# One joined load for both layouts of v, and fillers in the first halves only: linear attention, a token-mixing block and a gated block on one core

## The chip, the cores and the metric

The kernel runs on one core of a Trainium2 chip. Its engines work side by side, each through its own list of instructions: TensorE (matmuls; PE in the profile, PEld its weight loads), VectorE (DVE), ScalarE (ACT), GpSimd (POOL), and SyncE (SP), which issues the transfers. The metric is the device time of one execution in microseconds; lower is better.

## The reference, cut to what matters

Three blocks follow each other, for a batch of 4, 8 heads of 48 (384 channels) and 768 positions, all in float32:

```python
f = 1.0 / (1.0 + np.exp(-f_logit))
for t in range(S):                                   # per batch and head
    state = f[t][:, None] * state + outer(k[t], v[t])
    y[t] = q[t] @ state
theta = x @ w_theta                                  # x: y, heads side by side
y = w_tok_r @ (x * cos(theta)) + w_tok_i @ (x * sin(theta))
u = x + y
x2 = u + maximum(u @ w_ch, 0)
h = maximum(x2 @ w_in, 0)                            # 1024 wide: u, v
out = (u * (w_spatial @ layer_norm(v) + b_spatial)) @ w_out
```

## The kernel before

**Attention in chunks.** The recurrence is worked out in 12 chunks of 64 positions. A unit `u` is a pair of heads of one batch; there are 4 units in a batch, 16 in all. For a unit, `att_w` (or `half_w`) makes the outer products of k and v per chunk (tile `pw`), VectorE scans them into the state after each chunk (`cu`, later `cb`), `att_s` makes the scores of q and k inside each chunk (tile `psc`), which VectorE masks into `sc`, and `att_x` (or `half_x`) adds q times the state and the masked scores times v (tile `px`) and writes the result X. Every fourth row of the head pairs' tiles carries dimensions of a fourth pair, which are gathered by transfers into `kp` and `qp`; the fourth unit of each batch reads those.

v is needed in two layouts: with 128 positions on the partitions for the outer products (`VN`, tile names vn0 and vn1, from the array `vu`), and with 64 positions of either head of the pair for px (`VC`, vc0 and vc1, from `va`). Each layout has two tiles that alternate over units, and each is loaded by a transfer of its own: `half_load` (two transfers of 144 KB) and `att_load` (two of 288 KB).

**The first batch in halves.** Units 0 to 3 are worked on in two halves of 384 positions (h = 0 and h = 1), so that the work starts when half of the data is there: decay products on VectorE and ScalarE, transposes of k (tile `pt`), then `half_att`. Before each half's px, `warm` puts four matmuls of the identity (fillers, `px<-ident`) on TensorE; at the start 16 more (`pt<-ident`). A float32 matmul shows as two records, so a group of four fillers is eight records, and the eight groups are 64. The fillers' results are not used.

**Mixing and the rest.** `p1_theta` makes theta (`pth`), `p1_z` its sines and cosines times X (`z`), `p1_acc` multiplies by the token weights (`acc`), `p1_h` by w_ch (`hh`). Token weights arrive in twelve loads of 768 KB into a tile `ws` of two buffers (`ws<-tok_dram`), which ScalarE and VectorE convert to float32 (`tk`); w_theta comes through the same tile (`ws<-wt_dram`, converted into `ft`). From about 348 us on the gated block runs, batch by batch (`pv`, `pu`, `pg`, `po`).

**What sets the order.** Everything up to about 348 us is planned: the program's instructions are numbered as units in the order in which they are written (a whole group of matmuls is one unit), and the table `LINE` gives for each engine (T, V, A, G, and Q for SP's queue) the order in which it does its units. An engine works through its list strictly in that order, so an instruction that waits holds all behind it. A semaphore wait is added for each dependence on another engine. All data transfers of the planned stretch go through the one queue of SP. All instructions are recorded under line 259, in the helper that calls the engine; tiles tell them apart.

Of the kernel before, what the change touches and what calls it, by code (L numbers as in the profile page):

```python
# [10 lines left out]
F32 = mybir.dt.float32  # L11
# [10 lines left out]
P = 128  # L22
# [58 lines left out]
    ],  # L81
# [18 lines left out]
    ],  # L100
# [19 lines left out]
    ],  # L120
# [1247 lines left out]
```

## Time and profile before

| | before |
|---|---|
| median of 3 runs | 595.83 us (594.65 to 596.77) |
| profiled execution, its own time | 598.03 us |
| its span, first to last instruction | 596.3 us |
| TensorE busy | 581.0 us, 97% |
| VectorE busy | 452.0 us, 76% |
| ScalarE busy | 352.8 us, 59% |
| GpSimd busy | 29.1 us, 5% |
| granted TensorE clock, mean | 0.997 of full speed |

The span is what the trace covers; the profiled execution's own time has 1.7 us more around it. The profiled execution is one run, the median is over others. Busy shares are means over stages with different limits, and TensorE's records overlap, since the ends of matmuls are modelled: the start of one record to the start of the next says more than the length of one.

### The profile page before, as it was taken

Reading aid. Unit: us, or ns where it says so; the run is one execution under the profiler, and the core shown is the slowest. Engines: PE = TensorE matmul, PEld = TensorE weight load, DVE = VectorE, ACT = ScalarE, POOL = GpSimd, SP = SyncE. Lnnn points to the kernel's source line nnn. Section 1 sums busy time; section 2 is a strip of 40 time slices with the busy share of each in tenths; the row PEclk is TensorE's granted clock in tenths of the full one; section 3 lists DMA queues with packets and bytes.
Section 4 is the critical chain, followed back from the end, with each engine's and each line's share of the span. In section 5 each row is a group of like instructions: output and inputs, shape, how many; then the busy total and the mean of one; then the engine's idle time right before and its main releaser. Section 6 shows DMA issues by size and latency. Waiting matters only on the chain.

```text
span 596.3 us, 14184 instructions
## 1 busy us (share of the span) xinstructions
PE 581.0 (97%) x5750; PEld 533.3 (89%) x5750; DVE 452.0 (76%) x816; ACT 352.8 (59%) x683; POOL 29.1 (5%) x95
## 2 busy tenths in 40 slices
PE   7899998999999999999999999999999999999995
PEld 6776676877999999999999989999999999999995
DVE  6898998899887777764868587983968396839681
ACT  7798896598877888754664146623642364246421
POOL 5320110000000000000000000000000000000000
PEclk9999999999999999999999999999999999999998
DMA  7779966686978887778789999896049604940422
GB/s 240 209 240 333 281 200 250 226 287 210 304 240 307 271 311 247 256 249 282 244 282 320 338 354 299 288 373 212 1 139 373 203 1 147 371 145 0 158 89 78
DMA packets 68585, 139.44 MB, mean 234 GB/s; under 512 B 6496, under 2 KB 40800, under 8 KB 68512
## 3 DMA queue, kind: packets, MB, share of 16 engines
q1 hardware_dynamic: 68368, 138.36, 68.9%
q8 instruction: 47, 0.77, 0.6%
q14 instruction: 26, 0.21, 0.1%
q10 hardware_dynamic: 144, 0.10, 0.1%
HBM read 104.20 MB, written 31.85 MB: 228 GB/s over the span
## 4 chain that ended last, share of the span: by engine, by line
PE 91%; DMA 3%; DVE 2%; issue 1%; ACT 1%; SPq 1%; POOL 0%; DVEq 0%; ACTq 0%; POOLq 0%
PE acc L259 27%; PE pg L259 15%; PE po L259 9%; PE pu L259 8%; PE pv L259 8%; PE hh L259 6%; PE pth L259 6%; PE px L259 3%; PE psc L259 3%; PE pw L259 2%; PE pt L259 2%; DMA ws<-tok_dram 1%; SPq L259 1%; DMA k<-kd_dram 1%; DVE icp L259 1%
## 5 line engine op out<-in xcount | busy, mean ns | idle before, releaser
L259 PE MATMUL acc<-tk,z 128*128 128x384 f32 x792 | 172.4, 369 | 0.0
L259 PEld LDWEIGHTS acc<-tk,z 128*128 128x128 f32 x792 | 138.3, 189 | 15.8
L259 PE MATMUL pg<-sp,vn 128*128 128x384 f32 x504 | 88.0, 336 | 0.0
L259 PEld LDWEIGHTS pg<-sp,vn 128*128 128x128 f32 x504 | 87.4, 188 | 0.0
L259 PE MATMUL po<-wo,gt 128*128 128x384 f32 x288 | 51.3, 338 | 0.0
L259 PEld LDWEIGHTS po<-wo,gt 128*128 128x128 f32 x288 | 50.8, 188 | 0.0
L259 PE MATMUL pu<-x,wi 128*128 128x384 f32 x288 | 50.7, 335 | 0.0
L259 PEld LDWEIGHTS pu<-x,wi 128*128 128x128 f32 x288 | 50.1, 188 | 0.3
L259 PE MATMUL pv<-wi,x 128*128 128x512 f32 x216 | 49.8, 390 | 0.0
L259 PEld LDWEIGHTS pv<-wi,x 128*128 128x128 f32 x216 | 40.5, 188 | 8.2
L259 PE MATMUL hh<-uT,wc 128*128 128x384 f32 x216 | 41.9, 341 | 0.6 <-DVE uT L259 0.4
L259 ACT ACTIVATE gt<-g 128x384 fp32r<-128x384 f32 x32 | 16.7, 523 | 43.1 <-DVE g L259 42.5
L259 PEld LDWEIGHTS hh<-uT,wc 128*128 128x128 f32 x216 | 37.7, 188 | 1.6 <-DVE uT L259 0.9
L259 DVE TENSOR_TENSOR vn<-vr,vn 128x768 fp32r<-128x768 f32 x24 | 22.9, 955 | 16.1 <-ACT vn L259 15.8
L259 ACT ACTIVATE vn<-vr 128x768 fp32r<-128x768 f32 x24 | 20.2, 844 | 20.4 <-PE pg L259 17.9
L259 PE MATMUL pth<-wh,xT 128*128 128x384 f32 x108 | 31.9, 350 | 0.0
L259 DVE BATCH_NORM_STATS2 st<-vr 128x6 f32<-128x512 f32 x24 | 16.1, 687 | 19.6 <-ACT vr L259 19.6
L259 PE MATMUL px<-vc,sc 64*64 64x48 f32 x768 | 27.1, 220 | 0.2
L259 ACT ACTIVATE ws<-ws 128x768 f32<-128x768 f32 (+2 forms) x28 | 20.7, 738 | 10.4 <-DMA ws<-wo_dram 4.2
L259 ACT ACTIVATE oo<-po 128x384 f32<-128x384 f32 (+1 forms) x24 | 11.6, 482 | 24.8 <-PE po L259 23.7
L259 ACT ACTIVATE sn<-sn 128x384 f32<-128x384 f32 x48 | 24.3, 520 | 2.9 <-DVE sn L259 2.7
L259 PEld LDWEIGHTS px<-vc,sc 64*64 64x64 f32 x768 | 24.7, 140 | 0.5 <-DMA vc<-va_dram 0.3
(141 smaller groups left out, 1055.0 us busy)
## 6 DMA issues: line engine op xcount, KB each, us to landing
sp<-wpd SPq DMA_DIRECT2D x56, 576.0 KB, 5.9
tk<-tkp SPq DMA_DIRECT2D x48, 384.0 KB, 5.0
ws<-tok_dram SPq DMA_DIRECT2D x12, 768.0 KB, 5.9
tkp<-tk SPq DMA_DIRECT2D x24, 384.0 KB, 5.0
tkd<-tk SPq DMA_DIRECT2D x12, 384.0 KB, 5.7
x2d<-xt SPq DMA_DIRECT2D x24, 192.0 KB, 4.5
ws<-tkd SPq DMA_DIRECT2D x12, 384.0 KB, 4.9
xs<-x2d SPq DMA_DIRECT2D x12, 384.0 KB, 3.9
```

The source lines that it names most:

```text
L259: r = f(*a, **k)
```

## The change

The two tiles of v become one tile `VW` for each of the two buffers, of [128, 2, 12, 48]: the second index is the half of the positions; of the twelve slots, 0 to 5 hold the layout for the outer products (three position blocks for each head of the pair), 6 to 11 the layout for px (six chunks). The host-side array `vw` holds both layouts in that order, so that a half load and a whole load are one transfer each (288 KB and 576 KB), of one contiguous stretch per partition. The number of issues falls by 20 (8 half loads and 12 whole loads), the bytes stay the same.

`half_x` calls `warm` only for h = 0, so that four groups of fillers out of eight are gone.

The table `LINE` is a new one: 24 numbers fewer (20 loads, 4 groups of fillers), all later numbers shifted, and another order. Matched unit by unit, its lists hold the same remaining units on every engine. The mean shift of a unit is about two places on TensorE, four on VectorE, on ScalarE and in SP's queue. In the part up to the end of the second halves, what changes most is:

| unit | place before | place after |
|---|---|---|
| SP: loads of k, second halves, units 1 and 2 | 33, 39 | 17, 18 |
| SP: three loads of w_theta | 18, 23, 35 | 11, 23, 32 |
| SP: first three loads of token weights | 43, 45, 58 | 36, 37, 48 |
| SP: load of v for unit 2, first half (vn; vc) | 19; 27 | 21 (joined) |
| SP: load of v for unit 3, first half (vn; vc) | 30; 31 | 31 (joined) |
| ScalarE: first conversion step of tok loads 1, 2, 3 | 74, 84, 96 | 64, 74, 89 |
| VectorE: the three later steps of tok load 1 | 62, 63, 65 | 59, 60, 64 |
| VectorE: mask of unit 3, first half | 37 | 40 |
| TensorE: token matmuls of the first batch ahead of the last half px | 2 groups | 4 groups |

On TensorE the first group of fillers goes behind unit 0's scores, where it stood ahead of them. The diff, with the table's lines left out but for the start of the lists of T and Q:

```diff
 LINE = {
     "T": [
-        45, 46, 47, 48, 49, 50, 51, 52, 53, 61, 54, 55, 56, 57, 82, 58, 59, 60, 95, 100, 91, 101, 121, 128, 132, 137, 144, 138, 148, 153, 154, 159,
+        45, 46, 47, 48, 49, 50, 61, 51, 52, 53, 54, 82, 55, 56, 57, 58, 59, 60, 94, 90, 99, 100, 120, 126, 130, 135, 141, 136, 145, 150, 151, 155,
...
     "Q": [
-        13, 65, 14, 66, 15, 104, 125, 88, 67, 89, 105, 106, 126, 172, 64, 193, 232, 30, 141, 86, 173, 84, 35, 63, 124, 87, 142, 123, 85, 157, 158,
+        13, 65, 103, 14, 66, 15, 88, 168, 189, 67, 30, 105, 104, 124, 226, 64, 190, 227, 169, 170, 139, 63, 35, 123, 86, 122, 315, 85, 84, 87, 154,
...
-        self.VN = [a1.tile([P, 2, NT, D], F32, name=f"vn{i}") for i in range(2)]
-        self.VC = [a1.tile([P, NC, D], F32, name=f"vc{i}") for i in range(2)]
+        self.VW = [a1.tile([P, 2, NC, D], F32, name=f"vw{i}") for i in range(2)]
...
     def half_load(self, u, h):
         w = u % 2
-        self.Q.dma_start(out=self.VN[w][:, :, 3 * h : 3 * h + 3], in_=self.a["vu"][u][:, :, 3 * h : 3 * h + 3])
-        self.Q.dma_start(out=self.VC[w][:, 6 * h : 6 * h + 6], in_=self.a["va"][u][:, 6 * h : 6 * h + 6])
+        self.Q.dma_start(out=self.VW[w][:, h], in_=self.a["vw"][u][:, h])
...
-        Q, sc, v, st = self.att_kq(u)[1], self.SC[u % 2], self.VC[u % 2], self.st[u, h]
+        Q, sc, v, st = self.att_kq(u)[1], self.SC[u % 2], self.VW[u % 2], self.st[u, h]
         ps = [self.bank("px") for _ in range(2)]
-        self.warm(ps[0])
+        if h == 0:
+            self.warm(ps[0])
...
-                T.matmul(o, lhsT=sc[r, C * c : C * c + C], rhs=v[r, c], start=(c == 0), stop=True)
+                T.matmul(o, lhsT=sc[r, C * c : C * c + C], rhs=v[r, c // 6, 6 + c % 6], start=(c == 0), stop=True)
...
-        self.T.matmul(out, lhsT=self.KT[r, o : o + (C - 1) * step + 1 : step], rhs=self.VN[u % 2][r, i, n], start=True, stop=True)
+        self.T.matmul(out, lhsT=self.KT[r, o : o + (C - 1) * step + 1 : step], rhs=self.VW[u % 2][r, n // 3, 3 * i + n % 3], start=True, stop=True)
...
     def att_load(self, u):
         w = u % 2
-        self.Q.dma_start(out=self.VN[w], in_=self.a["vu"][u])
-        self.Q.dma_start(out=self.VC[w], in_=self.a["va"][u])
+        self.Q.dma_start(out=self.VW[w], in_=self.a["vw"][u])
...
+    rows = v2.reshape(B * NP, 2, 2, NT // 2, P, D).transpose(0, 4, 2, 1, 3, 5).reshape(B * NP, P, 2, NT, D)
+    cols = v2.reshape(B * NP, 2, 2, NC // 2, C, D).transpose(0, 1, 4, 2, 3, 5).reshape(B * NP, P, 2, NC // 2, D)
...
-        "vu": c(v2.reshape(B * NP, 2, NT, P, D).transpose(0, 3, 1, 2, 4)),
-        "va": c(v2.reshape(B * NP, 2, NC, C, D).transpose(0, 1, 3, 2, 4).reshape(B * NP, P, NC, D)),
+        "vw": c(np.concatenate([rows, cols], 3)),
```

## Rows read from the trace of the kernel before

**Rows 1.** Stretches: us, busy us and count by engine, granted clock, DMA share, GB/s.
```profile
30.00:55.00 25.00, 23.62 (x408) 17.77 (x407) 22.92 (x35) 21.19 (x49) 3.45 (x10) 1.00 0.82 282
55.00:100.00 45.00, 43.44 (x750) 30.58 (x751) 43.31 (x59) 38.22 (x71) 5.81 (x12) 1.00 0.82 269
100.00:348.00 248.00, 247.64 (x2780) 230.58 (x2776) 186.83 (x278) 166.28 (x293) 5.76 (x23) 1.00 0.81 272
```

**Rows 2.** TensorE's waits, whole span: us together, times, the longest.
```profile
PE px L259 <- DVE cu L259: 2.4, 4, 1.2
...
PE psc L259 <- issue: 1.6, 1, 1.6
```

**Rows 3.** Timeline of TensorE: start us, us, form, count [idle before, releaser].
```profile
2.33 3.88 PE L259 MATMUL pt<-ident 128*128 128x128 f32 x18 [2.33 <-POOL ident masks.py:199]
...
13.77 0.30 PE L259 MATMUL px<-vc,sc 64*64 64x48 f32 x8
...
29.80 1.06 PE L259 MATMUL px<-ident 128*128 128x128 f32 x8
30.71 2.20 PE L259 MATMUL pth<-ft,xt 128*128 128x384 f32 x6
33.02 0.39 PE L259 MATMUL px<-cu,qp 64*64 64x48 f32 x8
...
38.48 1.05 PE L259 MATMUL px<-ident 128*128 128x128 f32 x8
39.47 0.39 PE L259 MATMUL px<-cu,qp 64*64 64x48 f32 x8
...
43.63 1.05 PE L259 MATMUL px<-ident 128*128 128x128 f32 x8
44.90 0.39 PE L259 MATMUL px<-cu,qp 64*64 64x48 f32 x8 [0.21 <-DVE cu L259]
...
50.07 1.05 PE L259 MATMUL px<-ident 128*128 128x128 f32 x8
51.05 0.39 PE L259 MATMUL px<-cu,qp 64*64 64x48 f32 x8
...
54.84 0.55 PE L259 MATMUL pt<-ident,k 128*128 128x128 f32 x3 [0.59 <-ACT X L259]
```

**Rows 4.** The chain that ended last: start us, us, what.
```profile
35.26 0.86 PE psc L259 x22
...
43.09 7.06 DMA ws<-tok_dram
```

**Rows 5.** Timeline of SP's queue: issue start us, its us, transfer.
```profile
5.62 0.43 SPq L259 DMA_DIRECT2D vc<-va_dram  x1
...
11.71 0.57 SPq L259 DMA_DIRECT2D vn<-vu_dram  x1
...
17.37 0.53 SPq L259 DMA_DIRECT2D vc<-va_dram  x1
...
48.10 0.40 SPq L259 DMA_DIRECT2D vc<-va_dram  x1
```

**Rows 6.** Timeline of VectorE: start us, us, form [idle before, releaser].
```profile
29.74 0.36 DVE L259 TENSOR_SCALAR ft<-ws 128x384 uint32<-128x384 uint32 x1 [0.31 <-ACT ws L259]
...
31.63 0.56 DVE L259 TENSOR_TENSOR k<-k,icp 128x384 f32<-128x384 f32 x1 [0.35 <-DMA k<-kd_dram]
32.11 0.85 DVE L259 TENSOR_TENSOR_SCAN cu<-cu 128x336 f32<-128x336 f32 x1
...
41.32 0.96 DVE L259 SCALAR_TENSOR_TENSOR tk<-ws,tk 128x768 uint32<-128x768 uint32 x1
...
51.11 0.56 DVE L259 TENSOR_SCALAR tk<-ws 128x768 uint32<-128x768 uint32 x1 [1.26 <-ACT ws L259]
```

**Rows 7.** DMA issues: transfer, count, KB each, median us to landing.
```profile
vc<-va_dram SPq DMA_DIRECT2D x12, 288.0 KB, 5.8
...
vc<-va_dram SPq DMA_DIRECT2D x8, 144.0 KB, 4.0
```

More of the change, by code (lines that the diff above doesn't have):

```diff
@@ L619, in att_x @@
         A, T, pr = self.A, self.T, u % NP
-        Q, sc, v, st = self.att_kq(u)[1], self.SC[u % 2], self.VC[u % 2], self.st[u]
+        Q, sc, v, st = self.att_kq(u)[1], self.SC[u % 2], self.VW[u % 2], self.st[u]
         ps = [self.bank("px") for _ in range(2)]
@@ L630, in att_x @@
                 r = slice(64 * i, 64 * i + 64)
-                T.matmul(o, lhsT=sc[r, C * c : C * c + C], rhs=v[r, c], start=(c == 0), stop=True)
+                T.matmul(o, lhsT=sc[r, C * c : C * c + C], rhs=v[r, c // 6, 6 + c % 6], start=(c == 0), stop=True)
         for i in range(2):
```

121 rows, old and new, of the table LINE are left out of this document.

## The prediction

> **What bounds the kernel now.** First the page's slices, then the stretches of [rows 1]. From 100 us on TensorE is busy 247.64 of 248 us, and from 55 to 100 us 43.44 of 45: there the time is the sum of TensorE's instructions. Before 55 us it is another kernel: from 30 to 55 us TensorE is busy 23.62, VectorE 22.92 and ScalarE 21.19 of 25 us, and they hand small pieces to each other. This change takes nothing out of TensorE's work after 55 us, so what it brings is what the stretch before 55 us becomes shorter, less what waits a new order makes later.
>
> Then TensorE's waits: all that the profile names are small, 2.4 us for VectorE's scans (cu) in four waits and 1.6 us with no releaser, in one [rows 2], 2.3 us at the very start and 0.59 us for ScalarE's X [rows 3]. So little is to be had from waits; but TensorE's busy time before 55 us holds fillers, which do no work. The chain [rows 4] says what set the pace there: TensorE's own work from 35.26 us, then the third tok load, issued at 43.09 us and landing 7.06 us later; behind it come ScalarE's conversion and a table load, and at 54.84 us the transpose [rows 3] from which TensorE runs nearly without a gap. TensorE's timeline [rows 3] shows the fillers of the second halves and what follows each, SP's queue [rows 5] the issues, and VectorE's timeline [rows 6] where VectorE stood still.
>
> **The change, part by part.**
>
> *Fillers of the second halves.* Four groups go, each four matmuls (eight records). From the start of a group to that of its successor [rows 3]: 30.71 - 29.80 = 0.91 us, 39.47 - 38.48 = 0.99, 44.90 - 43.63 = 1.27 less the wait of 0.21 = 1.06, and 51.05 - 50.07 = 0.98; 3.94 us together. What of it is on the path:
> - First group: the theta matmuls behind it come 0.91 us earlier, but the px behind those began at 33.02 us, when the scan of VectorE that ran from 32.11 to 32.96 us was done [rows 3, 6]. I take 0; ends 0 and 0.91.
> - Second: its px ran at once, and the chain lies on TensorE from 35.26 to 43.09 us [rows 4]. I take 0.99; ends 0 and 0.99.
> - Third: its px waited for a scan, so TensorE gains only what VectorE is ahead by then. VectorE stood still for 0.31 us (for the conversion of w_theta) and 0.35 us (for k's load) at 29.7 and 31.6 us [rows 6]; both loads are issued earlier now (below), so 0.66 us, say 0.7. Ends 0 and 1.06.
> - Fourth: its px ran at once, 0.98, but the transpose at 54.84 us waited 0.59 us for ScalarE [rows 3], which came late through the third tok load [rows 4]. So 0.98 counts only if that load is earlier too. Ends 0 and 0.98.
>
> *One load in place of two.* 20 issues go from SP's queue. Nine of them are vc loads before 50 us, 0.43, 0.43, 0.53, 0.55, 0.43, 0.43, 0.53, 0.38 and 0.40 us of issue, 4.1 us together (the first, one of the dearest and the last stand in [rows 5]). The joined half load has the size of a whole load of before, 288 KB, which for vc took 5.8 us to landing where a half took 4.0 [rows 7], so the outer products' v may land 1.8 us later. What hides it: among TensorE's waits none of pw for a load of v is named, and the first unit's pw has the start fillers before it. Cover gone, it would be 1.8 us once, at the start.
>
> *The queue's new order.* The second-half loads of k go from places 33 and 39 to 17 and 18, the w_theta loads come a little earlier, the first three tok loads from 43, 45 and 58 to 36, 37 and 48. The third tok load needs the buffer that the first one's conversion frees (41.32 + 0.96 = 42.28 us, [rows 6]); its conversion on ScalarE stands ten places earlier, the three steps on VectorE three, three and one. In before VectorE then stood still for 1.26 us until 51.11 us [rows 6]: as much can the load come earlier before another thing is late. That removes ScalarE's lateness: 0.59 us of TensorE's wait at 54.84, and the fourth filler's 0.98 counts.
>
> *A wait that is added.* The joined tile is free only when px of two units earlier is done; the old vn only needed pw. For unit 2 the vn load went out at 11.71 us, vc at 17.37 us [rows 5]; unit 0's px began its last eight at 13.77 us and ended at 14.07 [rows 3]. In the new list this load stands at place 21; 20 issues at some 0.5 us, with a wait for the first product of q between, bring SP there at about 12 us (an estimate from [rows 5]: before, the 19th goes out at 11.71 us). SP then waits about 2.1 us, and behind it stand the gathers of kp, the second w_theta load and the gathers of qp. But at 14.1 us SP had in before issued 22 entries, two of them vc loads; the new list has 20 issued then. So the queue is level, and VectorE now has three more instructions (a product, a first step of the conversion, a scan) ahead of the mask that needs kp, together nearly 2 us by the like of them in [rows 6]. I take 0; ends 0 and 2.1 us of loss.
>
> *The order elsewhere.* The planned stretch is reshuffled to 348 us (mean shift two places on TensorE, four on VectorE and ScalarE). What it could gain there is the idle time of TensorE, 1.56 us from 55 to 100 and 0.36 us to 348 [rows 1]. What it could lose is new waits while VectorE has 1.7 us of slack in 45 us [rows 1]; the dearest price at hand for a late VectorE is 2.4 us in four waits [rows 2]. I take 0 from ends of 1.9 gained and 2.4 lost.
>
> Sum: 0 + 0.99 + 0.7 + 0.98 + 0.59 = 3.26, say 3.3 us. The profiled execution took 598.03 us (span 596.3 and 1.7 us around it), which is 2.2 us over the median 595.83 of the runs; the sum gives it 594.7 us, and the median 592.5 us.
>
> **The clock, which speaks against the change.** The granted clock reads 1.00 (2.4 GHz) in all stretches from 30 to 348 us [rows 1]. What the lower of the two levels, 1.2 GHz, costs can be seen at the very start: 18 filler records took 3.88 us, 0.216 us each, where the eight at 29.80 us took 0.114 us each [rows 3]. The Trainium skill (TensorE: Matmul & The Clock Gate, Part 1: The HAM clock gate) says that the throttled state is the default one and that only TensorE's activity keeps the clock up; by it a stretch emptied of fillers is where the clock could fall. The trace agrees in its first records. In the stretch concerned TensorE is busy 23.62 of 25 us [rows 1]; without 3.9 us of fillers 19.7 us of dense small matmuls and wide theta matmuls are left, so I expect it to hold.
>
> **The rivals.**
> - *VectorE sets the pace.* It is busy 22.92 of 25 us from 30 to 55 us [rows 1], and runs from 31.63 to 49.85 us back to back (27 instructions; [rows 6] has the first and the standstill at the end). If it doesn't get ahead, the fillers' time turns into TensorE's waits for scans: the second counts half, the others nothing, and the tok load alone gives 0.59. Gain up to 1.8 us, say 1.1: 594.7 us. For it: two of the four px waited for a scan. Against it: VectorE's own standing still of 0.31, 0.35 and 1.26 us came from loads, which all go out earlier.
> - *More is gained.* All of 3.94 and the 0.59, 4.5 us, and part of the 1.56 us that TensorE stands still between 55 and 100 us: under 591.3 us. For it: 1.6 us of that is a wait for nothing that the profile names [rows 2], so another order may be without it. Against it: the first group's time is had only with an earlier scan.
> - *The joined load holds the queue* (the other side). Place: unit 2's load at place 21 of SP's queue, and again unit 3's. Price: 2.1 us. It decides from the point where kp lands later than now by more than the nearly 2 us of work that VectorE has ahead of unit 3's mask; VectorE then stands still and all that follows is later. With the filler terms lost to the same late VectorE: 595.83 + 2.1 = 597.9 us. Against it: the count of entries above.
> - *The clock falls* in one stretch between two removed groups: from 29.80 to 38.48 us that is 8.7 us of work at half pace, 8.7 us more: 592.5 + 8.7 = 601.2 us.
> - *The change doesn't do what it says* can't well be: the fillers and the issues are instructions that are no longer there.
>
> **How the numbers follow.** A difference under 0.3% (1.8 us here) can't be told from none: faster means under 594.0, slower over 597.6. Forecast (gain of 1.8 to 4.5 us): 0.52, at 592.5. More gained: 0.10. VectorE sets the pace: 0.24, at 594.7, just inside "same". Queue held: 0.09, and clock: 0.05, both slower. So faster 0.62, same 0.24, slower 0.14. The forecast's own range is 591.3 to 594.0. For 8 in 10 the range goes down into the larger gain (all terms at their good ends, 3.94 + 0.59 + 1.56 = 6.1 us, give 589.7) to 590.2, and up over VectorE's case and some new waits (594.7 and most of the 2.4 us that new waits may cost) to 596.6; the slower cases and the last end of the larger gain are left out.
>
> **What would show it.** Right: px<-ident with 32 records in place of 64; the third tok load issued by 41.8 us or earlier; the transpose of k that came at 54.84 us about 3 us earlier against the work done by then; granted clock 1.00 from 30 to 55 us; TensorE's waits before 55 us no larger together than before. Wrong: TensorE's waits for cu grown by 2 us or more (VectorE's case); SP idle from 12 to 14 us and VectorE idle behind it before 27 us (the queue's); records between 30 and 50 us at twice their pitch (the clock's); or a gain at 55 us that is gone by 348 us, given back as new waits between 55 and 200 us, which is what I know least about.

## The result and the profile after

The changed kernel is slower: 599.79 us median (598.86 to 601.44, 6 runs) beside 596.3 us for the kernel before on the same chip (594.65 to 597.05, 6 runs), a ratio of 1.0065, 95% interval 1.0043 to 1.0086. Forecast was 592.5 us; the range to 596.6 us does not hold it. The profiled execution took 599.35 us, its span 597.5 us.

The stretches first, of the changed kernel, with two short ones around 254 us added (columns as in [rows 1]):

```profile
30.00:55.00 25.00, 24.46 (x408) 17.05 (x401) 23.99 (x36) 20.66 (x47) 2.74 (x15) 1.00 0.79 284
55.00:100.00 45.00, 43.92 (x841) 30.84 (x840) 42.52 (x60) 39.12 (x72) 3.53 (x8) 1.00 0.73 246
100.00:348.00 248.00, 244.24 (x2667) 228.50 (x2665) 184.49 (x275) 164.50 (x290) 11.41 (x22) 0.99 0.79 269
248.00:254.60 6.60, 4.40 (x130) 3.71 (x133) 2.51 (x4) 1.65 (x4) 0.00 (x0) 1.00 0.98 339
254.80:258.00 3.20, 3.20 (x69) 3.08 (x65) 1.36 (x1) 1.09 (x3) 0.00 (x0) 0.50 1.04 409
```

From 30 to 100 us TensorE is busier than in [rows 1], with 32 filler records fewer. From 100 to 348 us it is busy 244.24 us where it was 247.64, and at 254.80 us its granted clock is 0.50, the lower of its two levels. Its waits over the whole span say what came in (us together, times, the longest; before: [rows 2]):

```profile
PE pw L258 <- DMA vw<-vw_dram: 2.4, 2, 2.2
...
PE px L258 <- DVE cu L258: 1.5, 3, 0.6
PE pt L258 <- DVE k L258: 1.2, 1, 1.2
PE hh L258 <- DVE xt L258: 1.0, 1, 1.0
PE acc L258 <- DVE tk L258: 1.0, 2, 0.8
PE acc L258 <- DMA tk<-tkp: 0.8, 1, 0.8
```

The first, hh's, the larger of tk's and tkp's lie at 251, 351, 134 and 222 us, where the kernel before has no wait above 0.4 us. The fillers' places, on TensorE's timeline (before: [rows 3]):

```profile
30.15 2.20 PE L258 MATMUL pth<-ft,xt 128*128 128x384 f32 x6
...
32.61 0.39 PE L258 MATMUL px<-cu,qp 64*64 64x48 f32 x8
...
39.92 0.39 PE L258 MATMUL px<-cu,qp 64*64 64x48 f32 x8
...
50.72 0.39 PE L258 MATMUL px<-cu,qp 64*64 64x48 f32 x8
...
53.96 0.82 PE L258 MATMUL pt<-ident,k 128*128 128x128 f32 x6
```

No px waits for a scan at the three places shown, and the third tok load is issued at 40.40 us (43.09 in [rows 4]). So far this looks like the forecast. The wait at 251 us, first on TensorE, then in SP's queue:

```profile
250.24 1.31 PE L258 MATMUL acc<-tk,z 128*128 128x384 f32 x6
253.73 1.69 PE L258 MATMUL pw<-vw,kt 64*64 64x48 f32 x48 [2.18 <-DMA vw<-vw_dram]
```

```profile
232.60 0.38 SPq L258 DMA_DIRECT2D X<-wp_dram  x1
242.24 0.49 SPq L258 DMA_DIRECT2D qp<-q  x1
...
246.79 0.38 SPq L258 DMA_DIRECT2D vw<-vw_dram  x1
```

The joined load of unit 15 stands behind a gather of qp, which reads a product that VectorE ends only at 242.21 us:

```profile
241.26 0.95 DVE L258 TENSOR_TENSOR q<-q,cw 128x768 f32<-128x768 f32 x1
```

Issued at 246.79 us, the load lands 6.9 us later. In before the vn load of that unit went out ahead of its gather, and only vc came later:

```profile
237.01 0.42 SPq L259 DMA_DIRECT2D vn<-vu_dram  x1
...
243.28 0.49 SPq L259 DMA_DIRECT2D qp<-q  x1
...
244.98 0.41 SPq L259 DMA_DIRECT2D vc<-va_dram  x1
```

The wait at 351 us is one of VectorE's order (its timeline, then TensorE's):

```profile
349.99 0.56 DVE L258 TENSOR_TENSOR wt<-X 128x384 f32<-128x384 f32 x1 [0.86 <-DMA wpd<-X]
350.58 0.56 DVE L258 TENSOR_TENSOR X<-X 128x384 f32<-128x384 f32 x1
...
351.81 0.55 DVE L258 SCALAR_TENSOR_TENSOR xt<-hh,xt 128x384 f32<-128x384 f32 x1
```

```profile
352.41 0.80 PE L258 MATMUL hh<-uT,wc 128*128 128x384 f32 x3 [1.03 <-DVE xt L258]
```

VectorE stands at an instruction that needs a transfer, and the addition for which TensorE waits is queued behind it.

**Where the lead went.** Let each TensorE record other than fillers count with the mean start-to-start time of its kind (steps in which the engine stood idle left out); both kernels then have the same work. Against the profile of before, the changed kernel begins the same work earlier (-) or later (+) by, in us:

```
us in before      55     100     240     260     340     360
changed         -3.5    -4.8    -3.4    +0.3    +0.3    +1.5
```

The two kernels do the work in different orders, so the first figures hang on the weights: with medians in place of means it is 4.1 us ahead at 55 us and 2.9 at 240; from 260 us on nothing changes. So the changed kernel is 3.5 to 4.1 us ahead at 55 us, where 3.3 were forecast; 3.2 to 3.7 us go between 240 and 260 us (2.2 of wait, the rest at half clock) and about 1.2 at 351 us. One caution, which the experiments bear out: before's profile lies 1.7 us over its median, and the changed one had, as it turned out, the best start of all its kind.

### The profile page after: what moved, and what is told of

It reads as the page before. It is cut to its first block, busy times and chain, and to the rows that moved or that the text cites. A ratio compares the mean times of both kernels' runs of the same rounds, so it can differ in the third digit from the quotient of the medians.

```text
span 597.5 us, 14081 instructions
## 1 busy us (share of the span) xinstructions
PE 578.3 (97%) x5718; PEld 529.9 (89%) x5718; DVE 450.9 (75%) x816; ACT 354.1 (59%) x683; POOL 33.9 (6%) x95
## 4 chain that ended last, share of the span: by engine, by line
PE 76%; DMA 10%; DVE 5%; ACT 4%; issue 1%; SPq 1%; POOL 0%; ACTq 0%; DVEq 0%
PE acc L258 19%; PE pg L258 15%; PE po L258 8%; PE pu L258 8%; PE pv L258 8%; PE hh L258 5%; PE pth L258 4%; PE px L258 3%; DMA vw<-vw_dram 2%; PE psc L258 2%; DMA wpd<-X 2%; DMA ws<-tok_dram 2%; PE pw L258 2%; PE pt L258 2%; DVE tk L258 1%
## 5 line engine op out<-in xcount | busy, mean ns | idle before, releaser
L258 PE MATMUL px<-vw,sc 64*64 64x48 f32 x768 | 27.2, 220 | 0.0
L258 DVE TENSOR_TENSOR z<-sn,z 128x768 fp32r<-128x768 f32 x18 | 17.2, 956 | 12.6 <-ACT z L258 12.5
```

Of the source, the lines that this page charges most:

```text
L258: r = f(*a, **k)
```

## The experiments

Each was timed against the kernel before on its own chip, so ratios can be compared and bare medians less well (v15_look2 and v15_look3 are one execution each). "Old order" and "new order" are the tables `LINE` of the two kernels.

| kernel | median us | ratio to before, 95% interval |
|---|---|---|
| changed kernel | 599.79 | 1.0065, 1.0043 to 1.0086 |
| nofill_old | 596.80 | 0.9997, 0.9980 to 1.0014 |
| after_fill | 603.45 | 1.0102, 1.0082 to 1.0122 |
| joined_old | 600.98 | 1.0064, 1.0046 to 1.0082 |
| after_v15 | 600.77 | 1.0059, 1.0037 to 1.0081 |
| v15_look2, v15_look3 | 598.78, 599.79 | one execution each |
| hybrid | 596.92 | 0.9999, 0.9979 to 1.0019 |
| hybrid84 | 601.26 | 1.0092, 1.0065 to 1.0120 |
| newlate | 604.59 | 1.0138, 1.0115 to 1.0162 |
| after_split | 613.28 | 1.0295, 1.0270 to 1.0320 |
| after_fix | 597.87 | 1.0019, 0.9998 to 1.0040 |
| fix_no15 | 600.14 | 1.0062, 1.0041 to 1.0082 |
| v15_351 | 598.91 | 1.0043, 1.0022 to 1.0065 |
| after_fix2 | 596.13 | 0.9983, 0.9960 to 1.0005 |
| fix_fill | 597.55 | 1.0008, 0.9994 to 1.0023 |
| fix_split | 596.64 | 0.9994, 0.9978 to 1.0011 |
| fix2_split | 595.22 | 0.9984, 0.9967 to 1.0001 |
| split_start | 594.18 | 0.9947, 0.9926 to 0.9967 |

**The two edits alone, in the old order.** nofill_old takes the four groups of fillers out and nothing else:

```diff
-        self.warm(ps[0])
+        if h == 0:
+            self.warm(ps[0])
```

> The kernel before with its own order and its two loads of v; only the four groups of fillers of the second halves are gone. Theory 1 (the fillers' time is gained before 55 us, and the new kernel loses it again later to new waits): a gain of 1 to 3.3 us, 593.0 to 595.3 us, since the second group's 0.99 us lies on TensorE's chain and the others need earlier loads. Theory 2 (VectorE sets the pace before 55 us and the fillers were cover): 595.5 to 597 us, TensorE's waits for the scans grown by about what the fillers took.

Measured 0.9997, with 0.17% (1.0 us) either way: none of the 2.7 us that the prediction's sum gives to the fillers can be seen. Its waits from 10 to 56 us and the four px on its TensorE show why (before: [rows 2, 3]):

```profile
PE px L249 <- DVE cu L249: 4.2, 6, 1.2
```

```profile
33.23 0.39 PE L249 MATMUL px<-cu,qp 64*64 64x48 f32 x8 [0.26 <-DVE cu L249]
...
39.45 0.39 PE L249 MATMUL px<-cu,qp 64*64 64x48 f32 x8 [0.58 <-DVE cu L249]
...
45.23 0.39 PE L249 MATMUL px<-cu,qp 64*64 64x48 f32 x8 [1.22 <-DVE cu L249]
...
50.55 0.39 PE L249 MATMUL px<-cu,qp 64*64 64x48 f32 x8
```

The first three px begin at 33.23, 39.45 and 45.23 us where they began at 33.02, 39.47 and 44.90: the fillers' time became waits for VectorE's scans. The fourth runs at once, 0.50 us earlier. The transpose of k that waited 0.59 us for ScalarE in before runs without a wait here, 0.87 us earlier, though the third tok load goes out later than in before (43.40 us, and 43.09): it lands after 5.4 us where it took 7.06 [rows 4].

joined_old keeps the old order and the fillers and joins the loads, each at vn's place or, where the tile is not free then, behind the px that frees it:

```diff
-        self.Q.dma_start(out=self.VN[w], in_=self.a["vu"][u])
-        self.Q.dma_start(out=self.VC[w], in_=self.a["va"][u])
+        self.Q.dma_start(out=self.VW[w], in_=self.a["vw"][u])
```

> The kernel before with its own order and all fillers, but with the joined load of v in place of the two, each at the old vn load's place, or behind the px that it has to wait for (nine of twenty are moved back so). Theory 3 (the joined load itself costs, because it is free only after px of two units earlier): unit 13's load can go out only at 176.8 us in place of 156.1, for outer products at 178.6 us; with 5.8 us to landing they are 4 us late, so 598.5 to 601 us. Theory 1 in the form that the new order's places alone make the late waits: 595.5 to 597 us.

Measured 0.64% or 3.8 us slower (1.1 either way). The unit that waits is unit 11, counted in the program (the expectation calls it 13). Its load can only go out once px of unit 9 has read the tile, and pw, which used to need vn alone, waits 3.32 us (TensorE, then the stretch behind it):

```profile
181.42 1.69 PE L248 MATMUL pw<-vw,kt 64*64 64x48 f32 x48 [3.32 <-DMA vw<-vw_dram]
```

```profile
182.00:184.90 2.90, 2.90 (x45) 2.72 (x38) 0.00 (x0) 1.70 (x4) 0.00 (x0) 0.50 0.96 339
```

The clock stands at 0.50 right behind this wait too.

**The fillers in the new order.** after_fill puts one group ahead of each of the four second-half px of the changed kernel (`warm` for both halves, and its four units in the list of T).

> The changed kernel with the four groups of fillers put back, each right ahead of its px; all else as changed. Theory 1: 2 to 4 us slower than the changed kernel's 599.8, so 601.8 to 603.8 us. Theory 2: the same as the changed kernel within 0.6 us, 599.2 to 600.4 us.

0.37% or 2.2 us slower than the changed kernel (1.7 either way), as if the fillers cost their time there. But its profile has waits of 1.4 to 1.6 us at 185, 256 and 353 us, far behind the fillers; fix_fill (below) is the same edit with some of the waits of this order taken away.

**The largest wait.** after_v15 moves unit 15's load ahead of the gather:

```diff
 "Q": ...
-        1386, 1496, 1156, 1139, 1155, 1171, 1170, 1189, 1186,
+        1386, 1496, 1189, 1156, 1139, 1155, 1171, 1170, 1186,
```

> The changed kernel with one load moved: unit 15's joined load of v goes out ahead of the gather of q (which waits until 242.2 us) in place of five places behind it. Theory 1: TensorE's wait of 2.2 us for that load at 251.5 us is gone and the time falls by about as much, 597.0 to 598.2 us. Rival: TensorE's next instructions wait for other late things there (token weights, the store of the gated block's weights at 352 us), 599.2 to 600.4 us.

The wait and the half clock are gone from its profile, which took 596.5 us, but that was the lowest of nine executions, and the median did not fall. Two more profiles of the same program:

> The changed kernel with unit 15's load moved ahead, a second profile of the same program, since its first one was the fastest of its executions. Theory D': another wait of 1 us or more, or the clock at half for 3.4 us, stands in it at a fixed place (600 to 602). Theory E': the places differ from one execution to the next.

> A third profile of the same program. Same expectations as for the second: one fixed place with Theory D', differing places with Theory E'.

Both kinds of thing stand in them: fixed places (0.8 and 0.7 us for tk at 136 us, 1.1 us for xt at 350 us in both) and things that differ. The same TensorE record, at 22.10 us in the first profile, begins 0.6 and 0.8 us later; and in v15_look2 alone the granted clock is 0.50 from 27.99 to 31.40 us, behind waits of 0.6, 0.9 and 0.5 us.

**Mixed orders.** hybrid and hybrid84 follow the new order to TensorE's 60th and 84th entry, then the old one; newlate is the mirror of hybrid; after_split is the new order whole; all four with two loads per unit. hybrid against the new order, in the numbering with two loads:

```diff
 "T": ...
-        409, 446, 293, 432, 340, 342, 386, 431, 411,
+        409, 446, 293, 431, 386, 340, 342, 432, 344,
...
```

> The new order up to the 60th unit of TensorE's list (the last group of two-sided products of the first image, about 51 us; the other four lists are cut where what those 60 units need ends), then the old order; two loads for each unit's v, no fillers in second halves. Theory A (the early new order gains the 3.3 to 4.3 us that the changed kernel is ahead at 55 us, and its late order and its joined loads lose them): 592.5 to 594.0. Theory B (a lead at 55 us melts later whatever the late order is, since the work behind it is paced by other engines): 596 to 597.5, the old kernel's time. Between them says that part of the lead lasts.

> As the kernel with the new order up to the 60th TensorE unit, but the new order is kept up to the 84th (about 62 to 78 us), then the old one. Theory A: the lead of after at 80 to 100 us is still 4.4 us, so 592 to 594 again. Theory B: 596 to 597.5. If this one loses what the shorter one gains, the loss of the late order begins before 80 us, which the traces do not show.

> The mirror of the kernel with the new order up to the 60th TensorE unit: the same units up to there in the old order, then the new order; two loads for each v, issued up to twelve places of SyncE's list ahead of the joined load's place for the first and at that place for the second; no fillers in second halves. Ten TensorE units that the old order had begun by then are put off to behind the 60th. Theory A (the late new order itself loses, without joined loads): 600 to 602, three to five us over the old kernel. Theory C (it is the joined load that loses, not the late order): 596 to 598.

> The changed kernel's order whole, but two loads for each v as in the old one: the second at the joined load's place, the first up to twelve places ahead of it on SyncE's list, where the buffer is free. Unit 15's first load then goes out ahead of the gather that held it. Theory C (the joined load costs about 4 us, as it did in the old order, and the new order gains the 3.3): 594 to 596. Theory A (the late new order loses by itself): 598.5 to 601, like the changed kernel.

hybrid took the old kernel's time (0.2% either way), as Theory B has it: the early part of the new order, without fillers and with two loads, gains nothing that lasts to the end under the old late order. The other three came out slower than either of their expectations and say little: hybrid84 has waits of 1.2, 1.2 and 1.9 us that end between 84 and 95 us, where the orders are joined; in after_split the first loads, as placed, delay others (TensorE waits 3.2 us for k at the start and 4.3 us for VectorE's sn at 40 us), and newlate waits 1.95 us for qp at 70 us. An order cut in two is not a clean experiment, since its cut has waits of its own.

**The named waits, one by one.** after_fix has three moves in the changed kernel: unit 15's load as above, and

```diff
 "Q": ...
-        1065, 1013, 1038, 1064,
+        1065, 1064, 1013, 1038,
 "V": ...
-        1485, 1550, 1551, 1583, 1498,
+        1485, 1498, 1550, 1551, 1583,
```

> The changed kernel with three moves, one for each TensorE wait that its trace shows behind 200 us: unit 15's joined load ahead of the query gather that held it (as in the kernel with that move alone), the load of one token weight tile two places earlier on SyncE's list (the wait of 0.97 us at 222 us), and one addition of VectorE's list ahead of two that wait for a weight load (the wait of 1.19 us at 351 us). Theory D (the waits named in the trace carry the loss): 593.5 to 595.5, under the old kernel, since the lead of 3 to 4 us at 55 us then stays. Theory E (typical executions lose the time at places that one profile does not show, as the kernel with the first move alone suggests): 598 to 600.

Measured 1.0019: 0.46% or 2.7 us come back, but it is not under the old kernel. fix_no15 is after_fix without the first move, v15_351 without the load's (1064), and after_fix2 has a fourth:

```diff
 "Q": ...
-        636, 590, 617, 658,
+        636, 590, 658, 617,
```

> The kernel with three moves without the first: unit 15's joined load stands behind the query gather again, as in the changed kernel; the other two moves stay. If the wait of 2.2 us at 251 us and the half clock behind it come in most executions: 3.7 us over the kernel with three moves, about 601. If they come in few of them, as the kernel with that move alone suggests (its median fell by nothing against the changed kernel): within 1 us of 597.9.

> The changed kernel with unit 15's load ahead of the gather and the one addition of VectorE's list moved, without the token load's move. Theory D (the traces' waits add up): the kernel with the first move alone showed 0.9 to 1.3 us of wait at 349 us in three profiles, so 1.0 to 1.3 us under its 600.8, and 0.4 us (the wait at 222 to 225 us) over the kernel with three moves, so between 598.3 and 599.7. Theory E (more than the waits goes with these moves): outside that.

> The kernel with three moves plus a fourth: the load of token weights that stands behind a query gather on SyncE's list (the gather is held for 6.7 us at 116 to 122 us) goes ahead of it; VectorE and then TensorE wait behind it at 135 us, 0.8 to 0.9 us in each of the five profiles of this order. Theory D (the named waits carry the loss): 0.8 us under the kernel with three moves, 596.5 to 597.3. Theory E (a wait taken away there turns up again later): the same 597.9.

The ratios go 1.0065, 1.0059, 1.0043, 1.0019, 0.9983 as the moves are added: 0.82% or 4.9 us in all, with about 1.8 us either way from the two intervals. This sum is clear of noise; most single steps are not. Unit 15's move gave 0.06% as the first (0.3 either way) and 0.43% as the last of three (fix_no15 beside after_fix, 0.29 either way); why so differently is not shown. v15_351 came out as Theory D has it, after_fix2 under both of its expectations, fix_no15 between its two. fix_no15's profile shows that the wait at 251 us does not always come. SP's queue, then TensorE:

```profile
247.49 1.33 SPq L248 DMA_DIRECT2D vw<-vw_dram  x1
```

```profile
253.72 1.66 PE L248 MATMUL pw<-vw,kt 64*64 64x48 f32 x48
```

The load is as late as in the changed kernel, pw begins at the same 253.72 us, and there is no wait: TensorE does the same record 2.3 us later than in the changed kernel at 240 us. So in this execution there was no lead for the wait to take back. It is one of the two faster of six, though (598.2 and 598.4 us, mean granted clock 0.999 and 0.998); the other four took 600.1 to 601.5 us at 0.993 to 0.995, where after_fix's twelve have 0.995 to 0.999. That fits a stretch at half clock in the four, but no profile shows one.

**The edits again, with some of the waits gone.** fix_fill is after_fix with the fillers back, fix_split after_fix with two loads, one directly behind the other at the joined load's place:

```diff
 fix_fill
-        if h == 0:
-            self.warm(ps[0])
+        self.warm(ps[0])
 fix_split
-        self.Q.dma_start(out=self.VW[w], in_=self.a["vw"][u])
+        self.Q.dma_start(out=self.VN[w], in_=self.a["vu"][u])
+        self.Q.dma_start(out=self.VC[w], in_=self.a["va"][u])
```

> The kernel with three moves with the fillers of the second halves put back, one ahead of each of the four groups of products. Theory F (in the new order the fillers cost their time, 2.7 us of the prediction's sum, wherever the waits behind them are): 600.0 to 601.5. Theory G (the 3.6 us between the changed kernel and the one with fillers came from shifted waits): 597.5 to 599.

> The kernel with three moves, with two loads for each unit's v again, both at the joined load's place, the one directly behind the other. It asks what the joining itself gives in the order made for it. If it gives nothing: within 0.5 us of the kernel with three moves. If one transfer saves issue time or lands earlier at the dense start: 1 to 2 us slower, as the mixed order with two loads started 1.3 us later at 23 us.

Neither edit gains or costs anything clear of noise: the fillers' return gives 1.0008 beside 1.0019 (0.26% either way), two loads 0.9994 (0.27% either way). Stretches of after_fix, then of fix_fill:

```profile
30.00:55.00 25.00, 23.45 (x428) 16.38 (x425) 23.06 (x35) 20.17 (x47) 3.35 (x13) 1.00 0.80 284
55.00:100.00 45.00, 43.55 (x798) 30.75 (x798) 42.46 (x60) 38.38 (x71) 4.55 (x10) 1.00 0.71 240
```

```profile
30.00:55.00 25.00, 25.00 (x457) 19.38 (x456) 22.88 (x35) 19.69 (x44) 2.98 (x13) 1.00 0.79 267
55.00:100.00 45.00, 44.29 (x769) 30.91 (x761) 41.84 (x58) 38.93 (x72) 3.85 (x10) 1.00 0.75 251
```

With the fillers TensorE never stands still from 30 to 55 us; without them it does so for 1.55 us. But the work itself comes earlier without them. These kernels have the same list for TensorE but for the fillers, so one record can be followed through all of them. The first px of the last second half begins at

```
changed kernel                                  50.72 us
same order, joined, no fillers (7 profiles)     51.93 to 53.83 (after_fix 52.74)
same order, joined, with fillers (2 profiles)   54.05 (fix_fill), 54.96 (after_fill)
```

after_fix is 1.3 us ahead of fix_fill there and at 57 us; at 150 us the two are level, and at 350 us fix_fill is 1.8 us ahead. So what the removed fillers gave early in this pair was taken back by waits behind 57 us, among them the 1.31 us at 80 us shown at the end of this document, which fix_fill does not have. The middle of the eight profiles without fillers is 53.1 us. The changed kernel's profile was the best of them; read alone, it made the early part look 2.4 us better than it usually is.

**The start.** fix2_split is after_fix2 with two loads; split_start has beside that the old order of TensorE's first 18 entries:

```diff
 "T": ...
-        45, 46, 47, 48, 49, 50, 61, 51, 52, 53, 54, 82, 55, 56, 57, 58, 59, 60,
+        45, 46, 47, 48, 49, 50, 51, 52, 53, 61, 54, 55, 56, 57, 82, 58, 59, 60,
```

> The kernel with four moves and two loads for each unit's v, the one directly behind the other: the candidate that may beat both. With three moves the two loads were 1.2 us under the joined load, and the fourth move was worth 0.8 us by the traces: 595 to 596, which is 0.2 to 0.3% under the old kernel. If the two gains do not add: 596 to 597.

> The kernel with four moves and two loads, with the first 18 entries of TensorE's list in the old order: the first transposes of k stand behind nine start fillers instead of six. In the new order TensorE waits 1.7 to 2.5 us there, and in nine of fourteen profiles its clock rises to full only at 9.6 to 13.2 us, where all four profiles with the old start have it from 5.7 to 7.5 us. Theory H (the wait among the start fillers delays the clock in part of the executions, and that costs 0.6 to 1 us each time): full clock from 5.7 to 7.5 us again, the median 0.3 to 0.8 us under the kernel with four moves and two loads, 594.4 to 594.9, and fewer of its executions above 596. Theory I (the start is hidden behind the loads of k and q anyway): the same 595.2.

split_start beats both kernels: 0.9947, 3.2 us under the old one, and 0.37% (2.2 us, about 1.6 either way) under fix2_split by the ratios, while the two medians, from different chips, are 1.0 us apart; its executions lie from 592.98 to 595.79 us, fix2_split's from 593.60 to 598.49. The start on TensorE, of after_fix2, then of split_start:

```profile
6.90 0.90 PE L248 MATMUL pt<-ident,k 128*128 128x128 f32 x3 [1.80 <-DVE k L248]
7.59 1.91 PE L248 MATMUL pt<-ident 128*128 128x128 f32 x8
```

```profile
6.52 0.55 PE L249 MATMUL pt<-ident,k 128*128 128x128 f32 x3 [0.56 <-DVE k L249]
6.90 1.06 PE L249 MATMUL pt<-ident 128*128 128x128 f32 x8
```

Eight filler records take 1.91 us at the lower level of the clock, 0.24 us each, and 1.06 at the full one. (The prediction's 0.216 us for the lower level came from 18 records whose last ran at the full level, from 5.71 us on.) Whether the gain is larger than the 0.3 to 0.8 us expected can't be told, and the one profile of split_start (its longest execution, with a wait of 1.5 us for qp at 11 us and the clock at half from 12.20 us) does not show where the gain comes from.

## Why the prediction was wrong, by its own steps

- **The fillers (0.99 + 0.7 + 0.98 of the 3.3 us): the first step that failed.** It took time saved before 55 us for time saved at the end. In the old order the removal is worth nothing that can be seen (0.9997, 1.0 us either way): there the rival "VectorE sets the pace", held at 0.24, was right, and three of the four removed groups met a scan a moment later, with TensorE and VectorE both busy more than 90% of that stretch [rows 1]. In the new order VectorE's standstills of 0.31, 0.35 and 1.26 us did go, as the prediction held against that rival, and the work came earlier; but in after_fix beside fix_fill the lead of 1.3 us was gone by 150 us, and the times are the same (1.0019 without, 1.0008 with). In the changed kernel itself the removal is worth 2.2 us (1.7 either way), close to the 2.67 forecast, so what it is worth hangs on the waits behind it.
- **The tok load (0.59): not shown.** The third load goes out 2.7 us earlier, VectorE's standstill of 1.26 us [rows 6] is gone, and TensorE's wait for X at the transpose of k too. But both are gone in nofill_old as well, where that load is issued 0.3 us later than in before and only lands sooner (5.4 us, not 7.06). So the new place in the queue need not be what removed them.
- **The order elsewhere (0, from 1.9 gained to 2.4 lost): failed, and its end was too near.** Four moves of one instruction each in the new order's later part and middle are worth 4.9 us together (1.8 either way). No step went through the queue behind 55 us; the prediction itself named new waits there as what it knew least about, and placed them between 55 and 200 us; the largest two behind 55 us came at 251 and 351 us.
- **The added wait of the joined load (0, from 0 to 2.1): right where it was looked at, but it was looked at only there.** SP stood 2.0 us for px ahead of unit 2's load (2.1 forecast), and TensorE's waits for vw at units 2 and 3 are 0.2 us. Unit 15 in the new order and unit 11 in the old one are the places that pay. Nor do the 20 issues saved show: with two loads the same order is no slower (0.9994 beside 1.0019, 0.9984 beside 0.9983).
- **The clock:** from 30 to 55 us it held in the changed kernel, as forecast, and the rival that a stretch without fillers lets it fall did not come true there. It fell behind a wait at 251 us, and cost not 8.7 but some 1 to 1.5 us (3.2 to 3.7 us of lead lost less 2.18 us of wait). The Trainium skill (TensorE: Matmul & The Clock Gate, Part 1: The HAM clock gate) has the throttled state as the default one, which activity releases. The falls behind waits agree with it. The same section says that the clock's rise at a start differs from run to run; the trace agrees (below).

Put together: a gain of 3.3 us that did not last to the end, and new waits in the new order, with what half clock follows them, that were taken as 0. That the loss lies in these waits rests on the four moves as a sum; how much each carries in a typical execution stays open, since one profile each shows waits that others have not. Open is also why the median of after_v15 stayed at the changed kernel's, and whether the old start alone would bring the joined load's kernel under the old one: it was tried only with the other moves and two loads.

## What to carry to other kernels

Before time taken off one engine counts, ask for each place what the next instruction there waits for: where two engines are both busy over nine tenths, as here, one's saving can become its wait for the other, and the cheapest test is to make that one edit alone. Then follow the time saved to the end of the kernel: a lead can be taken back by any later wait. Joining two loads ties the later use of one to the earlier need of the other, so walk through every unit with the queue in hand and not only the first ones. And compare a lead read from one profile with that of several profiles of like kernels: here one profile in eight was 2.4 us better than the middle by 53 us.

## What the runs showed of the hardware

- **A wait can cost the clock as well.** Behind waits of 2.2 us (changed kernel) and 3.3 us (joined_old) the granted clock is 0.50 for 3.41 us; so it is in newlate behind 1.95 and 1.27 us and in split_start behind 1.54. It is not certain: hybrid84 waited 1.91 us at 93 us and kept it, and after_fill kept it behind three waits of 1.4 to 1.6 us.
- **When the clock rises at the start varies.** With the old start the full level comes at 5.4 to 7.5 us in all five profiles. With the new one, where 1.7 to 3.6 us go by from the last filler ahead of the transpose of k to that transpose, it comes at 5.1 to 5.6 us in five profiles and at 9.6 to 13.2 us in ten (the expectation counted nine).
- **TensorE sometimes stands still with no releaser, perhaps for its instructions.** Several of its waits have none, 0.7 to 1.6 us long, most of them in dense groups of small matmuls (one of 1.56 us, in after_fill at 187.54 us, among wide ones). In after_fix, TensorE, and the packets on one queue from 79 to 81 us:

```profile
81.92 0.34 PE L248 MATMUL pw<-vw,kt 64*64 64x48 f32 x9 [1.31 <-issue]
```

```profile
q8 instruction: 1, 0.02, 3.4%
```

  The packet on this instruction queue (47 packets, 0.77 MB in the whole program, so 16 KB each) starts at 79.39 us. In before, such a packet starts at 96.36 us, 0.6 us ahead of the last matmul before the 1.6 us wait of [rows 2]; in nofill_old 0.6 and 1.1 us ahead of two. That the fetch is the cause was not tried by itself: most of the 47 packets have no such wait behind them. The Trainium skill (Runtime: NRT & Kernel Launch, Instruction fetch mechanics) has this fetch mostly hidden. These waits, in groups of matmuls every 17 to 31 ns, may be places where it is not. The wait at 80 us stands in all eight profiles of the joined new order without fillers, and in none of fix_fill, fix_split and fix2_split.
